# Normalised rows transposed by DMA on ScalarE's queue, and MLP pieces that run two behind the batch

## The chip, the cores and the metric

One core of a Trainium2 chip runs the kernel. The metric is the device time in microseconds of one execution, taken as the median of several runs; smaller is better.

## What is computed

Attention over 8 batches, 8 heads, 576 rows and 64 columns a head, with a causal mask and a bias from a running sum, and on its output a layer norm, a two-layer MLP with ReLU and a residual:

```python
scores = scale * q @ k.T
cum = cumsum(max(s, 0))
scores = where(causal, -1e9, scores + minimum(-(cum_i - cum_j), 0))
attn = softmax(scores)
x = concat_heads(attn @ v)                      # 8 x 576 x 512
xn = (x - mean(x)) / sqrt(var(x) + 1e-6) * g_ln
out = x + maximum(xn @ w_ch1, 0) @ w_ch2        # 512 -> 2048 -> 512
```

## The kernel before

**Slots.** The main loop runs over n = 0 to 63, one slot for each batch b = n // 8 and head h = n % 8. A slot computes the scores of its head (three PSUM banks `sa`, `sb`, `sc`, line 312, and for even h a small tile `sd`, line 347), takes their exponential on ScalarE into `er` (lines 323 and 358), masks on GpSimd (line 331), and then multiplies `er` of the head of two slots ago with V (`pv`, line 389, called by `pv_next`). The three score banks come from one PSUM pool of three buffers, so that the scores of a slot need the exponentials of the slot before to be done. VectorE divides by the row sums and writes the head's 64 columns into `xb` (512 rows of a batch) and `xm` (the last 64 rows, those of two batches in one 128-row tile).

**Normalisation.** When head 7 of a batch has gone through `pv`, which is in slot h=1 of the next batch, `ln_xn` (line 444) forms the normalised rows `xn` in bf16 for tiles t = 0 to 3 of 128 rows, and for odd batches for a fifth tile t = 4, the shared `xm`. The MLP needs them with the 512 columns on the partitions. `ln_tr` (line 478) does that: four TensorE transposes of 128x128 into a PSUM tile `trx` (line 484), and a copy by VectorE or ScalarE to `xT` or, for t = 4, `xTm` (lines 98 to 100). In slot h=2 of the next batch it handles tiles 0 and 1, in slot h=3 tiles 2, 3 and 4 (lines 822 to 827); for batch 7 it runs after the loop (line 842).

**MLP pieces.** `batch_units` puts 32 pieces of four matmuls of 512 columns each into a Python list `queue`: 16 of the first layer (`mlp1`, line 497; each ends in a ReLU to `hT` on ScalarE, or on VectorE for the first piece of a slot), then for each of four row tiles four quarters of the second layer (`mlp2`, line 515), of which the last ends in the residual sum `yo` on VectorE (line 524) and a DMA of 256 KB to the output on SyncE's queue (line 542). `run_units(n)` takes pieces from the list: in every slot one after the scores, one more after `sd`, and the rest after `pv`. The number per slot (line 809) is the length of the list over the slots to the next h=3, where the list is emptied (line 833) and the next batch's 32 pieces are put in. So the first layer takes slots h=4 to h=7, the second h=0 to h=3. A last chunk of 32 and some pieces handles the four `xm` tiles together.

**K and Q.** For batches 3 to 7, groups of four heads are loaded with SyncE's queue (`ld_rows`, line 164), cast on GpSimd (line 176) into 128-row tiles with the bias columns, and transposed into `kq` by five DMA transposes on SyncE's queue (`tr_rows`, line 186; the fifth has 64 rows). They are issued in slots h=4, 5 and 6 or h=0, 1 and 2 ahead of the group's first slot (h=0 or h=4). V is loaded on the same queue. The instructions of each engine and each issuing queue run in the order in which the program gives them; DMAs issued from SyncE and ScalarE rotate over eight completion semaphores, so each waits for the one issued eight before.

Of the kernel before, what the change touches and what calls it, by code (L numbers as in the profile page):

```python
# [15 lines left out]
P = 128  # L16
# [3 lines left out]
def kernel(  # L20
# [11 lines left out]
    nc = tc.nc  # L32
    B, H, S, D = q.shape
# [5 lines left out]
    NF = S // P  # L39
# [48 lines left out]
    xTm = const.tile([P, KD, 512], BF16, name="xTm")  # L88
# [7 lines left out]
    def copy_on(eng, out, in_):  # L96
        if eng == "act":
            nc.scalar.copy(out=out, in_=in_)  # L98
        elif eng == "dve":
            nc.vector.tensor_copy(out=out, in_=in_)  # L100
        else:
            nc.gpsimd.tensor_copy(out=out, in_=in_)  # L102
# [140 lines left out]
    def tr_pair(g):  # L243
        tr_kind("k", g)
        tr_kind("q", g)
# [29 lines left out]
    def qk_pair(g, k_engs, q_engs):  # L275
        tr_pair(g)
        evac_pair("k", g, k_engs)
        evac_pair("q", g, q_engs)
# [149 lines left out]
    xTs = {}  # L428
    xns = {}
# [48 lines left out]
    def ln_tr(b, t, eng="dve"):  # L478
        if (b, t) not in xns:
            return  # L480
        xn = xns.pop((b, t))
        tr = ps_t.tile([P, KD, P], BF16, name="trx", tag="tr")
        for kd in range(KD):
            nc.tensor.transpose(tr[:, kd, :], xn[:, kd * P : (kd + 1) * P], ident)  # L484
        if t < NF:
            dst = xTs[b][:, :, t * P : (t + 1) * P]
        else:
            dst = xTm[:, :, (b // 2) * P : (b // 2 + 1) * P]
        copy_on(eng, dst, tr)

    first_unit = [False]

    def mlp1(xT, fb):
# [60 lines left out]
    queue = []  # L554
    pend = []

    def run_units(n, dve_first=False):
        for i in range(n):
            if queue:
                first_unit[0] = dve_first and i == 0  # L560
                queue.pop(0)()
# [3 lines left out]
    def keep_warm(n):  # L565
        w = ps_t.tile([P, 512], F32, name="idle", tag="tr")
        for _ in range(n):
            nc.tensor.matmul(w, lhsT=zeros[:, 0:P], rhs=zeros, start=True, stop=True)
# [26 lines left out]
    for i in range(2):  # L595
# [5 lines left out]
        out=maskT,  # L601
        in_=maskT,
# [18 lines left out]
    for t in range(NT):  # L621
# [5 lines left out]
        out=c_in, in0=c_in, scalar1=0.0, scalar2=1.0 / scale, op0=ALU.max, op1=ALU.mult  # L627
    )
    nc.vector.tensor_tensor_scan(
        out=c_sc, data0=c_one, data1=c_in, initial=0.0, op0=ALU.mult, op1=ALU.add  # L630
# [44 lines left out]
    def pre(n):  # L675
        if n == 0:
            nc.vector.memset(mhalf, -0.5)
            ld_cast_pair(4)
        elif n == 1:
            ld_w1(1)  # L680
        elif n == 3:
            ld_cast_pair(5)
            for t in range(NT):
                ld_cast_v(1, t)
        elif n == 4:
            ld_w1(2)
            ld_w1(3)
        elif n == 7:
            ld_cast_pair(6)
            ld_w2(0)  # L690
            ld_cast_pair(7)
            ld_w2(1)
        elif n == 10:
            ld_w2(2)
            ld_w2(3)
        elif n == 12:
            nc.vector.memset(cT[:, :, 0, :, 0], -1.0)
            nc.vector.memset(cT[:, :, 1, :, 1:4], 1.0)
        elif n == 16:
            for r in rows:  # L700
                nc.gpsimd.memset(r[:, :, :, KA:P], 0.0)
        if n in PAIR_LOADS:
            ld_cast_pair(PAIR_LOADS[n])
        if n % 4 == 0 and 2 <= n // 4 + 1 < 2 * NPE:
            aug(n // 4 + 1, nc.sync)
        for gam in range(2 * NPE, NG):
            m = n - 4 * gam
            if m == -6:
                ld_rows(gam, 0), ld_rows(gam, 1)
            elif m == -5:  # L710
                cast_rows(gam, 0), cast_rows(gam, 1)
                ld_rows(gam, 2), ld_rows(gam, 3)
            elif m == -4:
                tr_rows(gam, 0), tr_rows(gam, 1)
                cast_rows(gam, 2), cast_rows(gam, 3)
                ld_rows(gam, 4)
            elif m == -3:
                tr_rows(gam, 2), tr_rows(gam, 3)
                cast_rows(gam, 4)
            elif m == -2:  # L720
                tr_rows(gam, 4)
        for nb in range(2, B):
            m = n - H * nb + (5 if nb == 2 else 7)
            if 0 <= m < NT:
                ld_v(nb, m)
            if 1 <= m <= NT:
                cast_v(nb, m - 1, "pool")

    def pv_next():
        pb, ph_ = pend.pop(0)  # L730
        pv(pb, ph_)
        if ph_ in (3, 5) or (ph_ == 7 and pb > 0):
            ln_stats(pb, ph_ // 2 - 1)
        elif pb == 0 and ph_ in (6, 7):
            ln_stats(0, ph_ - 4)
        if ph_ == 7:
            ln_open(pb)
            if pb == 0:
                ln_first()
                return  # L740
            for t in range({1: 3, B - 1: 1}.get(pb, NT)):
                ln_xn(pb, t)


    for n in range(BH):
        b, h = n // H, n % H
        pre(n)
        if n < 8:
            scores(b, h)
            if h in (1, 3, 5, 6):  # L750
                scores_d(b, h // 2)
            if h in (0, 2, 4):
                qk_pair(h // 2 + 1, ("dve", "dve"), ("act", "dve" if h < 4 else "act"))
            pend.append((b, h))
            if n == 7:
                pv_next()
                tr_pair(4)
                pv_next()
                evac_pair("k", 4, ("act", "act"))
                evac_pair("q", 4, ("act", "act"))  # L760
                trc = bias_tr()
                keep_warm(8)
                continue
            if n % 2 == 1 or n == 0:
                keep_warm(2)
            if n > 1:
                pv_next()
            if n == 6:
                pv_next()
            continue  # L770
        if n == 8:

            phs = [
                pool.tile([P, 512], F32, name="ph", tag=tag)
                for pool, tag in ((ps_m, "m"), (ps_m, "m"), (ps_s, "s"), (ps_s, "s"))
            ]

            def columns(t):
                cols = slice(t * P, (t + 1) * P)
                for fb, ph in enumerate(phs):  # L780
                    for kd in range(KD):
                        nc.tensor.matmul(  # L782
                            ph[:, cols],
                            lhsT=w1_bf[:, kd, fb * P : (fb + 1) * P],
                            rhs=xTs[0][:, kd, cols],
                            start=(kd == 0),
                            stop=(kd == KD - 1),
                        )

            for t in range(NF):  # L790
                ln_tr(0, t, "act" if t < 3 else "dve")
                if t > 0:
                    columns(t - 1)
            columns(NF - 1)
            for fb, ph in enumerate(phs):
                if fb % 2 == 0:
                    nc.scalar.activation(out=hT[:, fb, :], in_=ph, func=ACT.Relu)
                else:
                    nc.vector.tensor_scalar_max(out=hT[:, fb, :], in0=ph, scalar1=0.0)
            ln_first_rstd()  # L800
            queue += batch_units(0)[4:]
            scores(b, h)
            scores_d(b, h // 2)
            pend.append((b, h))
            run_units(1)
            continue

        end = next(m for m in (8 * i + 3 for i in range(2, B + 1)) if m >= n)
        nu = (2 if n < 16 else -(-len(queue) // (end - n + 1))) - 2
        if n in PAIRS:  # L810
            qk_pair(PAIRS[n], ("dve", "dve"), ("act", "act"))
        scores(b, h)
        run_units(1, True)
        if h % 2 == 0:
            scores_d(b, h // 2)
        run_units(1)
        if n > 9:
            pv_next()
        if n == 9:
            bias_rows(trc)  # L820
        pend.append((b, h))
        lt = {2: (0, 1), 3: (2, 3, 4)}.get(h, ()) if b > 1 else ()
        for t in lt:
            ln_tr(b - 1, t, "act" if b == 2 else "dve")
            if t != 1 and t != 4:
                run_units(1)
                nu -= 1
        if n == 2 * H + 2:
            for t in range(3, NT):
                ln_xn(1, t)  # L830
        run_units(nu)
        if b > 1 and h == 3:
            run_units(len(queue))
            queue += batch_units(b - 1)
    pv_next()
    run_units(3)
# [2 lines left out]
    for t in range(NT):  # L839
        ln_xn(B - 1, t + 1)  # L840
        run_units(1)
        ln_tr(B - 1, t, "act")
    run_units(len(queue))
    queue += batch_units(B - 1)
    queue += mixed_units()
# [30 lines left out]
```

## Time and profile before

| | |
|---|---|
| median of 5 runs | 368.45 us (368.0 to 368.88) |
| the profiled execution, its own time | 368.88 us |
| its span, first to last instruction | 367.2 us |
| granted TensorE clock | 1.00 |
| TensorE matmuls for the transposes of `xn` (line 484) | 144, on `trx` |
| copies out of `trx` | 23 on VectorE (415 ns), 13 on ScalarE (585 ns) |
| SyncE's DMA transposes into `kq` | 50, median issue 1.27 us |
| loop slots from n = 20 on, without a transpose of `xn` | 4.6 us each |

The profile is one execution as the hardware profiler recorded it. A row of the timeline gives start, duration, engine, source line, operation, output<-inputs, shape and count; brackets give the idle time of the engine before it and who ended it. PE is TensorE, PEld its weight loads, DVE VectorE, ACT ScalarE, POOL GpSimd, SP SyncE; a trailing q means the engine's queue that issues DMAs. Digits in the page's slices are the busy tenths of fortieths of the span. The landing of a DMA is read from the semaphore records of the trace: the last of its 16 increments.

### The profile page before, as it was taken

The numbers are of one execution on the slowest core, as the hardware profiler recorded it, in microseconds if no ns is written. First come the engines' busy times: TensorE is split into PE (matmuls) and PEld (weight loads), VectorE is DVE, ScalarE is ACT, GpSimd is POOL, SyncE is SP. The second block draws the span as 40 slices with busy tenths as digits, with TensorE's granted clock in tenths as the row PEclk, the third lists the DMA queues.
The fourth block names the chain that finished last, engine by engine and source line by source line (L and its number), as shares of the span: only waits on it lengthen the run. The fifth ranks groups of instructions, "written<-read, shape, count | busy, mean of one in ns | idle before, by whom it ended". The sixth has DMA issues, their size and how long they took to land.

```text
span 367.2 us, 8322 instructions
## 1 busy us (share of the span) xinstructions
PE 354.8 (97%) x3029; PEld 198.0 (54%) x3079; DVE 205.5 (56%) x539; ACT 194.2 (53%) x371; POOL 162.3 (44%) x441
## 2 busy tenths in 40 slices
PE   8898999999999999999999999999999999999995
PEld 3577565565555555555555555555555554444444
DVE  7597789795438453944385547743665483112211
ACT  5796988568743674357534753476337522501410
POOL 8864375748643746445744562555652101000000
PEclk9999999999999999999999999999999999999999
DMA  7999995579955989499969987798730011011013
GB/s 142 170 192 177 201 201 87 111 188 177 194 122 129 239 173 199 110 234 175 193 156 216 200 184 134 182 202 190 162 100 2 0 60 57 3 55 59 3 29 86
DMA packets 147981, 50.42 MB, mean 137 GB/s; under 512 B 134185, under 2 KB 143268, under 8 KB 147940
## 3 DMA queue, kind: packets, MB, share of 16 engines
q1 hardware_dynamic: 129364, 40.74, 51.2%
q0 software_dynamic: 18176, 8.62, 19.9%
q10 hardware_dynamic: 400, 0.52, 0.5%
q8 instruction: 24, 0.39, 0.4%
q14 instruction: 17, 0.14, 0.1%
HBM read 37.11 MB, written 9.44 MB: 127 GB/s over the span
## 4 chain that ended last, share of the span: by engine, by line
PE 84%; DVE 8%; ACT 3%; DMA 2%; issue 2%; ACTq 0%
PE ph L497 31%; PE py L515 30%; PE pot L389 7%; PE sc L312 4%; PE sa L312 3%; PE sb L312 3%; DVE xn L451 2%; PE trx L484 2%; DMA kq<-c 2%; DVE stats L423 1%; ACT er L323 1%; PE trqk L255 1%; ACT kq L98 1%; PE ph L782 1%; DVE xb L399 1%
## 5 line engine op out<-in xcount | busy, mean ns | idle before, releaser
L515 PE MATMUL py<-w_bf,hT 128*128 128x512 bf16 (+1 forms) x564 | 132.2, 373 | 1.6 <-DVE yo L524 0.4
L497 PE MATMUL ph<-xT,w_bf 128*128 128x512 bf16 x479 | 116.6, 379 | 1.1 <-DVE yo L524 0.2
L507 ACT ACTIVATE hT<-ph 128x512 bf16<-128x512 f32 x102 | 61.0, 598 | 62.8 <-PE ph L497 62.8
L515 PEld LDWEIGHTS <-hT 128*128 128x128 bf16 x592 | 53.5, 98 | 49.1 <-issue 0.9
L497 PEld LDWEIGHTS <-w_bf 128*128 128x128 bf16 x560 | 50.3, 97 | 51.7 <-issue 3.3
L323 ACT ACTIVATE er<-sa 128x512 bf16<-128x512 f32 x64 | 38.2, 597 | 70.4 <-PE sa L312 50.9
L331 POOL TENSOR_SCALAR_AFFINE_SELECT er<-er 128x128 bf16<-128x128 bf16 x216 | 59.4, 298 | 28.1 <-ACT er L323 28.0
L505 DVE TENSOR_SCALAR hT<-ph 128x512 bf16<-128x512 f32 x38 | 26.3, 692 | 54.6 <-PE ph L497 49.1
L176 POOL CAST rows<-rowtmp 128x512 bf16<-128x512 f32 (+1 forms) x50 | 30.5, 610 | 46.0 <-DMA rowtmp<-in_q_dram 42.8
L312 PEld LDWEIGHTS <-kq 68*128 68x128 bf16 x440 | 32.8, 97 | 26.6 <-DMA kq<-c 1.7
L389 PEld LDWEIGHTS <-er 128*128 128x128 bf16 x960 | 37.4, 98 | 14.2 <-issue 0.7
L389 PE MATMUL pot<-v_bf,er 128*128 128x65 bf16 x960 | 39.6, 193 | 0.3 <-PE sd L355 0.3
L323 ACT ACTIVATE er<-sc 128x512 bf16<-128x512 f32 x64 | 39.2, 613 | 0.0
L397 DVE RECIPROCAL rinv<-pot 128x5 f32<-128x5 f32 x64 | 12.3, 192 | 47.7 <-PE pot L389 47.4
L323 ACT ACTIVATE er<-sb 128x512 bf16<-128x512 f32 x64 | 38.4, 600 | 0.1
L524 DVE SCALAR_TENSOR_TENSOR yo<-py,rstd,xb 128x512 f32<-128x512 f32 x32 | 24.0, 748 | 25.5 <-PE py L515 18.6
L439 POOL TENSOR_TENSOR rstd<-rstd,mhalf 128x4 f32<-128x4 f32 (+1 forms) x8 | 8.8, 1097 | 44.7 <-DVE rstd L438 44.7
L399 DVE TENSOR_TENSOR xb<-pot,rinv 128x256 f32<-128x256 f32 x64 | 27.2, 425 | 2.2
L312 PE MATMUL sa<-kq 68*128 68x512 bf16 x64 | 24.4, 381 | 1.5 <-DMA kq<-c 1.2
L423 DVE BATCH_NORM_STATS2 stats<-xb 128x6 f32<-128x128 f32 (+2 forms) x100 | 25.3, 313 | 0.4
L312 PE MATMUL sc<-kq 68*128 68x256 bf16 (+1 forms) x208 | 25.2, 232 | 0.3
L102 POOL CAST v_bf<-vtmp 128x512 bf16<-128x512 f32 (+1 forms) x30 | 18.4, 614 | 14.5 <-DMA vtmp<-in_v_dram 13.2
(101 smaller groups left out, 331.4 us busy)
## 6 DMA issues: line engine op xcount, KB each, us to landing
out_dram<-yo SPq DMA_DIRECT2D x32, 256.0 KB
vtmp<-in_v_dram SPq DMA_DIRECT2D x24, 256.0 KB
rowtmp<-in_k_dram SPq DMA_DIRECT2D x40, 128.0 KB
rowtmp<-in_q_dram SPq DMA_DIRECT2D x40, 128.0 KB
w_bf<-in_moe_w_ch_dram POOLq DMA_DIRECT2D x8, 512.0 KB, 10.6
kp<-in_k_dram POOLq DMA_DIRECT2D x11, 144.0 KB, 6.1
qp<-in_q_dram POOLq DMA_DIRECT2D x11, 144.0 KB, 6.5
v_bf<-in_v_dram POOLq DMA_DIRECT2D x8, 128.0 KB, 8.5
```

Source lines behind the costliest of these rows:

```text
L176: nc.gpsimd.tensor_copy(out=r[0:pn, :, :, 0:D], in_=loaded.pop(("rows", gam, t))[0:pn])
L312: nc.tensor.matmul(a[:, c + a0 - q0 : c + a1 - q0], lhsT=k_cols(b, h, kb), rhs=cols, start=True, stop=not (pe_mask and diag),)
L323: nc.scalar.activation(out=e[:, o : o + 512], in_=a, func=ACT.Exp, scale=scale)
L331: nc.gpsimd.affine_select(out=e[:, o : o + P], in_=e[:, o : o + P], compare_op=ALU.is_ge, fill=0.0, base=0, pattern=[[1, P]], channel_mult ...
L389: nc.tensor.matmul(pot[:, t, :], lhsT=e[:, o : o + P], rhs=vv[:, kb, h, :], start=(kb == 0), stop=(kb == last),)
L399: nc.vector.tensor_tensor(out=xb[b][:, :, hs], in0=pot[:, 0:NF, 0:D], in1=rinv[:, 0:NF].unsqueeze(2).to_broadcast([P, NF, D]), op=ALU.mult,)
L423: nc.vector.bn_stats(out=st[b][:, t, part, :], in_=x[:, lo:hi])
L497: nc.tensor.matmul(ph, lhsT=w1_bf[:, kd, fb * P : (fb + 1) * P], rhs=xT[:, kd, :], start=(kd == 0), stop=(kd == KD - 1),)
L505: nc.vector.tensor_scalar_max(out=hT[:, fb, :], in0=ph, scalar1=0.0)
L507: nc.scalar.activation(out=hT[:, fb, :], in_=ph, func=ACT.Relu)
L515: nc.tensor.matmul(py[0], lhsT=hT[:, fb, t * P : (t + 1) * P], rhs=w2_bf[:, fb, c0:c1], start=(fb == 0), stop=(fb == FB - 1),)
L524: nc.vector.scalar_tensor_tensor(out=yo, in0=py[0], scalar=rs, in1=x[:, c0:c1], op0=ALU.mult, op1=ALU.add)
```

## The change

Tiles of batches 2 to 7 no longer go through TensorE: a new `ln_dma` takes an `xn` tile and issues one DMA transpose from ScalarE's queue, straight into `xT` or `xTm`. Batches 0 and 1 keep `ln_tr`. In the loop, tiles 0, 1 and 2 are issued at the end of slot h=2, tile 3 at the head of slot h=3 before its scores, tile 4 at the end of slot h=3; for batch 7, each tile is issued after the loop where its `ln_tr` was. In the built order of ScalarE's queue, tiles 0 to 3 stand together between the exponentials of h=2 and those of h=3, and tile 4 between those of h=3 and h=4. The pieces per slot are written out: four in each slot from n = 20, three in slots 23 and 27; the list is no longer emptied at h=3, so two second-layer pieces are left there and run first in slot h=4, and the first layer of the next chunk begins after that slot's `pv`.

```diff
+    def ln_dma(b, t):
+        if (b, t) not in xns:
+            return
+        if t < NF:
+            dst = xTs[b][:, :, t * P : (t + 1) * P]
+        else:
+            dst = xTm[:, :, (b // 2) * P : (b // 2 + 1) * P]
+        nc.scalar.dma_start_transpose(out=dst, in_=xns.pop((b, t)))
...
-        end = next(m for m in (8 * i + 3 for i in range(2, B + 1)) if m >= n)
-        nu = (2 if n < 16 else -(-len(queue) // (end - n + 1))) - 2
+        if n < 16:
+            nu = 2
+        elif n < 20:
+            nu = -(-len(queue) // (20 - n))
+        else:
+            nu = 3 if n in (23, 27) else 4
+        nu -= 2
+        if b > 2 and h == 3:
+            ln_dma(b - 1, 3)
...
-        lt = {2: (0, 1), 3: (2, 3, 4)}.get(h, ()) if b > 1 else ()
+        lt = {2: (0, 1), 3: (2, 3, 4)}.get(h, ()) if b == 2 else ()
         for t in lt:
-            ln_tr(b - 1, t, "act" if b == 2 else "dve")
+            ln_tr(b - 1, t, "act")
...
         run_units(nu)
+        if b > 2 and h == 2:
+            for t in range(3):
+                ln_dma(b - 1, t)
+        if b > 2 and h == 3:
+            ln_dma(b - 1, 4)
         if b > 1 and h == 3:
-            run_units(len(queue))
             queue += batch_units(b - 1)
...
         ln_xn(B - 1, t + 1)
         run_units(1)
-        ln_tr(B - 1, t, "act")
+        ln_dma(B - 1, t)
```

## The prediction

> **What bounds the kernel now.** I read the page's busy lines and slices first, then the chain of waits, TensorE's waits, the instruction groups by form, and last the timeline of one batch. The page:
>
> ```profile
> span 367.2 us, 8322 instructions
> PE 354.8 (97%) x3029; PEld 198.0 (54%) x3079; DVE 205.5 (56%) x539; ACT 194.2 (53%) x371; POOL 162.3 (44%) x441
> PE   8898999999999999999999999999999999999995
> ACT  5796988568743674357534753476337522501410
> DMA  7999995579955989499969987798730011011013
> ...
> PE 84%; DVE 8%; ACT 3%; DMA 2%; issue 2%; ACTq 0%
> ```
>
> TensorE is full in every slice from the sixth on, and no other engine is. TensorE's waits (who, for whom, us, times, longest) come to under 6 us in the whole span, mostly in the start:
>
> ```profile
> PE sa L312 <- DMA kq<-c: 1.2, 1, 1.2
> PE sd L347 <- ACT kq L98: 0.6, 2, 0.4
> PE trx L484 <- DVE xn L451: 0.5, 2, 0.3
> PE py L515 <- DVE yo L524: 0.4, 2, 0.2
> ```
>
> So a TensorE instruction taken out of the loop or the tail is time gained, unless what replaces it makes TensorE wait. The work in question, by form (count | busy us, mean ns | idle before), and SyncE's existing transposes (min/median/max ns):
>
> ```profile
> L484 PE MATMUL trx<-ident,xn 128*128 128x128 bf16 x144 | 13.8, 219 | 0.6 <-DVE xn L451 0.5
> L100 DVE COPY xT<-trx 128x512 bf16<-128x512 bf16 x21 | 8.1, 417 | 2.0 <-PE trx L484 1.6
> L98 ACT COPY xT<-trx 128x512 bf16<-128x512 bf16 x11 | 6.4, 585 | 14.3 <-PE trx L484 14.2
> ...
> L186 SPq DMA_TRANSPOSE kq<-rows x50: 1218/1274/2228, 83.0 to 267.5; - x50
> ```
>
> 219 ns is a pipelined duration; the rate is what counts. The timeline of batch 5 (slot h=2 starts at 186.28, h=3 at 191.36):
>
> ```profile
> 186.28 0.38 PE L312 MATMUL sa<-kq 68*128 68x512 bf16 x1
> ...
> 188.20 0.27 ACT L358 ACTIVATE er<-sd 64x128 bf16<-64x128 f32 x1
> ...
> 191.36 0.38 PE L312 MATMUL sa<-kq 68*128 68x512 bf16 x1
> ...
> 191.62 1.22 SPq L186 DMA_TRANSPOSE kq<-rows  x1
> ...
> 191.84 0.60 ACT L323 ACTIVATE er<-sa 128x512 bf16<-128x512 f32 x1 [3.36 <-PE sb L312]
> ...
> 194.21 0.39 PE L484 MATMUL trx<-ident,xn 128*128 128x128 bf16 x4
> ...
> 194.43 1.03 PE L515 MATMUL py<-w_bf,hT 128*128 128x512 bf16 x4
> ```
>
> Four transposes of one tile cost 194.43 - 194.21 = 0.22 us of TensorE. The slots agree: 4.63 us for even h and 4.58 for odd without such tiles, but h=2 takes 5.08 with two tiles (+0.45), h=3 5.02 with two (+0.44) and 5.62 with three (+1.04, of which 0.67 is the tiles and 0.37 is waiting, for DVE's yo among it). The bracket in ACT's row at 191.84 says that ACT had been idle 3.4 us: in h=2 and h=3 it has little but its exponentials.
>
> **What the Trainium skill says.** Page "DMA: Bandwidth & Descriptors", section "DMA Transpose (X-bar)", on two transposing streams in flight: transposes issued from SP and from ACT must not overlap; the later stream's first must wait for the earlier one's full completion. In the changed program's order ACT's first transpose of each batch does wait for SP's last kq transposes, and SP's next one for ACT's last. Only SP transposes in the kernel before, so its trace doesn't show the price. Same page, "Issuing engines are not separate DMA queues": all queues share the 16 DMA engines, so ACT's queue adds load and no bandwidth. The trace agrees in that transfers land later when the engines are full: SP's kq transposes land 2.7 to 5.7 us after issue.
>
> **The change part by part.**
>
> TensorE, removed: 4+5+4+5+4 tiles of batches 2 to 6 and 5 of batch 7, 27 tiles, 108 transposes: 27 x 0.223 = 6.0 us, all on the bound engine. With them go waits: 0.37 us in each of the two three-tile slots of that length (h=3 of batches 4 and 6) and 0.07 in the tail. Together 0.8; I count half, since yo still queues behind DVE's normalisation: 0.4.
>
> DVE, removed: 22 evacuations x 0.415 = 9.1 us, from the slots where it also normalises. ACT, removed: 5 x 0.585 in the tail. Neither bounds; they count only through the half of the waits above.
>
> ACT, added: 27 transpose issues, each of 4 column blocks of 128. SP's issue of 8 blocks takes 1.27 us, with 64 rows as with 128, so blocks set it; its plainest copy (out) takes 0.33 us. If the issue is all blocks, 0.63; if 0.33 is fixed, 0.33 + 4 x 0.117 = 0.80; if the count of blocks doesn't matter, 1.27. I take 0.75, ends 0.63 and 1.27. A value below nothing is excluded, since it is new work on this queue. What matters is the in-order queue: behind the four transposes stand the exponentials of slot h=3, and for these TensorE waits, since scores of h=4 reuse their three PSUM banks. In batch 5, counted from h=2's start T2 = 186.28: ACT ends h=2's exponentials at T2+2.2, xn of tiles 0 to 3 ends at +1.3, +2.3, +3.2, +4.1. ACT's first issue waits for SP's transpose of the group's last 64 rows. Before, that one was issued only at T2+5.3, because SP stood behind an output write that waited for yo. In the new order the output write ahead of it is one whose yo is made before the normalisation, since the MLP runs half a slot later; then SP's own work sets it: two transposes from T2-2.8 to T2-0.1, one v load and one write, then issue at about T2+1.1, landing 2.7 us later, T2+3.8. Then 0.3 for the several waits and 4 x 0.75: ACT is free at T2+7.1. Exponentials of h=3 would start at T3+0.48 = T2+5.1 in a slot of 4.6, so they lag 2.0 us. The third one ends at T3+2.05 today and its bank is wanted at T3+5.0: 2.95 us of slack. Cost nothing, by 0.95 us. If that cover is gone, each us beyond it costs a us a batch, five times. The fifth tile (odd batches) goes out behind h=3's exponentials with 0.75 and delays h=4's by no more than what ACT's idle 3 us absorb.
>
> Landing of xT: the fourth tile is issued by T2+7.1, lands 3 to 5 us later, at the latest T2+12.1. First use is the first MLP-1 piece, now after two pieces and the PV of h=4: T2+9.2+3.2 = T2+12.4. Just hidden at the long end; at 3 us by 2 us. In the tail: xn of tile 3 ends at 301.8 before, issue and landing give 305.5; 15 pieces of 0.86 us from the last PV at 294.3 last until 307.3. Hidden.
>
> SP: nothing is added, but its next rows and transposes wait for ACT's landings (to T2+10). Before, SP's first kq transpose of the next group went at T2+17.3 in batch 4 (163.6 against 147.96) through the yo block, and the group's last landed 1.0 us ahead of its use. SP loses the block of up to 5.7 us and gains a wait that is shorter: nothing, most likely some slack. POOL: same instructions.
>
> DMA engines: 27 x 128 KB in 256-byte packets, 512 each, 13,824. The 129,364 packets of SP's queue took 51.2% of 367.2 us on 16 engines, 23 ns each, so an estimated 20 us of all 16: mean share from 72% to some 78%. Loads have slack in slots, so I count nothing; it lengthens landings.
>
> Pacing: every slot from 20 on still runs four pieces of 0.86 us (three in 23 and 27, which leaves two behind), 32 a batch, so TensorE's sum is the same. ReLU pieces move half a slot away from the transposes: the cover for ACT's issue.
>
> Sum, against the profiled execution: 368.88 (span 367.2 and 1.7 around it) - 6.0 - 0.4 = 362.5. The median of the runs, 368.45, is 0.43 below it: 362.1.
>
> **The rivals.** (1) Partly eaten: the issue costs about 1.0 us, or SP's last transpose lands 1 us later than worked out; ACT is free at T2+8.1, lag 3.0, and every fuller batch oversteps: 0.5 to 0.8 us in each of five, 3 us back: about 365. For it: an SP issue took up to 2.2 us when the DMA engines were full. Against: that was for twice the blocks.
>
> (2) No change: issue at SP's full 1.27 us. ACT is free at T2+9.2, lag 4.1, overstepped by 1.15 in five batches = 5.8 us: 367.9, no change by the bound below; 0.1 us more a batch and it is 368.4.
>
> (3) Slower: ACT's queue blocks behind SP's landing. Its place is the first transpose of each batch; if SP's last kq transpose lands 5.0 instead of 2.7 us after issue (the longest of the 128-row ones is 5.7), because the DMA engines now carry more, and issues cost 1.0, ACT is free at T2+10.4, lag 5.3, and TensorE stalls for a bank by 5.3 - 2.95 = 2.35, 11.8 us in five batches: 362.1 + 11.8 = 373.9. (xT, landing later too, is wanted later by the same stall.) It decides from a delay of 2.25 us beyond my T2+7.1 on: then 1.3 us x 5 pays back the 6.4. For it: both queues are in order and wait for each other. Against: the 64-row transposes, which are the ones waited for, landed within 2.7 to 3.0 us in all ten groups.
>
> **How the numbers follow.** Forecast 0.62 at 362.1 (own range 361.2 to 364); rival 1 0.14; rival 2 0.06; rival 3 0.18. Faster by over 0.2%, about what this measurement can tell from no change: 0.62 + 0.14 = 0.76; within it 0.06; slower 0.18. The range goes from 361.0 (all waits gone, 0.4 better, and some more) to 370.5, which takes in rivals 1 and 2 and the near part of 3; some 0.15 is left above and 0.04 below.
>
> **What would show it.** Right: 36 instead of 144 transposes on TensorE, slots h=2 and h=3 of batches 3 to 7 at 4.6 us; ACT's transposes near 0.75 us each, its exponentials of h=3 late by some 2 us and TensorE's waits still under 1 us per batch; SP's last small transpose issued before ACT needs it. Wrong: TensorE waits at scores of h=4 for ACT, or at MLP-1 pieces for a DMA into xT, or at the next group's scores for kq; issues of 1.2 us or more on ACT; a tail that waits for batch 7's landing.

## The result: the gain on TensorE came, and was given back with more

| | before | after |
|---|---|---|
| median | 368.28 us (46 runs, 367.57 to 370.3) | 370.58 us (26 runs, 367.20 to 374.04) |
| after / before, 95% interval | | 1.0051 [1.0037, 1.0065] |
| the profiled execution, its own time | 368.88 | 372.53 |
| its span | 367.2 | 370.8 |

So 2.3 us slower where 6.4 us faster was forecast, at the upper end of the range, 370.5. The ratios here and below compare fast runs alone: five of the 26 runs after, 373.0 to 374.0 us, count as slow, and by the ratio the kernel is 1.9 us slower. The kernel after also spreads more, 6.8 us against 2.7. The profiled executions differ by 3.65 us, more than the medians; the sums below are made against them.

The page of the kernel after, busy lines and slices:

```profile
span 370.8 us, 8187 instructions
PE 352.5 (95%) x2924; PEld 192.8 (52%) x2971; DVE 196.4 (53%) x517; ACT 191.3 (52%) x366; POOL 161.6 (44%) x441
PE   8898999999999999989997999999989999999995
PEclk9999999999999999999999999999989999999999
DMA  8999994679999999999899899999730033001003
```

The slices that had stood at 9 without a break from the sixth to the last but one now have three holes: an 8 in the 18th (158 to 167 us), a 7 in the 22nd (195 to 204) and an 8 in the 30th (269 to 278). Those are the slots h=3 and h=4 of batches 4, 5 and 7. TensorE's waits (who, for whom, us, times, longest) name two that weren't there:

```profile
PE sa L312 <- ACT er L323: 3.9, 3, 2.4
PE ph L507 <- DMA xT<-xn: 2.4, 2, 1.6
```

Both are on the list of signs under which the forecast is wrong: scores of h=4 that wait for ScalarE's exponentials, and first-layer pieces that wait for a transposed tile. (Line 507 is `mlp1`, 497 in the kernel before; the change shifts what follows it by ten lines and more.) What is behind the first stands in the answer for line 499, the new DMA transposes on ScalarE's queue (count, then min/median/max ns of one issue):

```profile
L499 ACTq DMA_TRANSPOSE xT<-xn x24: 1204/1234/1408, 111.2 to 304.9; - x24
L499 ACTq DMA_TRANSPOSE xTm<-xn x3: 1231/1237/1267, 155.3 to 306.3; - x3
```

An issue of four column blocks takes 1.23 us, as long as SyncE's of eight.

**Where the time went, batch by batch.** Most slots are as forecast: 4.63 and 4.58 us, h=2 and h=3 with the rest. I measured each slot from its first score to the next slot's and took the excess over that. T2 is again the start of slot h=2, and the batch is that of the slot; the tiles belong to the batch before it.

| batch | ScalarE issues tiles 0 to 3 | exponentials of h=3 start | tile 3 lands | excess, us | what TensorE waited for |
|---|---|---|---|---|---|
| 3 | T2+2.1 to 7.5 | T2+7.6 | T2+12.4 | 1.28 | the tile, at the first piece of `mlp1` |
| 4 | T2+3.0 to 8.6 | T2+8.7 | T2+14.5 | 2.44 | the tile |
| 5 | T2+5.8 to 11.1 | T2+11.2 | T2+13.7 | 3.12 | score bank, so ScalarE |
| 6 | T2+2.1 to 7.4 | T2+7.5 | T2+11.5 | 0.18 | next to nothing |
| 7 | T2+4.6 to 9.9 | T2+10.0 | T2+11.0 | 1.89 + 1.69 | score bank; 1.69 is put down to a halved clock, below |

Together 10.6 us. With 6.0 us of transposes and 0.8 us of waits gone, 367.2 - 6.8 + 10.6 = 371.0, against a span of 370.8.

Batch 5 in the timeline (start, us, engine, line, operation; brackets: idle before, releaser; T2 = 185.65, h=3 starts at 190.28, h=4 at 197.45):

```profile
186.66 2.74 SPq L186 DMA_TRANSPOSE kq<-rows  x1
190.28 0.38 PE L312 MATMUL sa<-kq 68*128 68x512 bf16 x1
191.41 5.29 ACTq L499 DMA_TRANSPOSE xT<-xn  x4
196.81 0.60 ACT L323 ACTIVATE er<-sa 128x512 bf16<-128x512 f32 x1 [8.96 <-POOL v_bf L102]
197.45 0.38 PE L312 MATMUL sa<-kq 68*128 68x512 bf16 x1 [2.43 <-ACT er L323]
```

Read it from the top. SyncE's last `kq` transpose of the group needs 2.74 us to issue (min 1.2) and lands at T2+5.6. Only then does ScalarE issue its four, 5.29 us without a break: in every batch of the trace its first transpose starts only after SyncE's last one has landed, here by 0.2 us. ScalarE has done nothing else for 8.96 us, yet the exponentials of h=3, whose scores have lain ready since about 191, start at 196.81: 6.05 us later than the T2+5.1 of an undisturbed slot. The forecast's rule for what that costs was lag less 2.95 us of bank slack: 3.10, and the slots of this batch are 3.12 us too long. In batch 7 it gives 4.84 - 2.95 = 1.89, and 1.89 is left of the 3.58 measured there when the clock's 1.69 is taken off.

Batch 4 is the other kind; its lag of 3.6 us would cost 0.6, but the tile lands later still, and TensorE waits for it:

```profile
160.93 1.89 PE L507 MATMUL ph<-xT,w_bf 128*128 128x512 bf16 x8 [1.63 <-DMA xT<-xn]
```

And in batch 7, behind a gap of 1.23 us on TensorE at 273.23, the clock halved. Three stretches of that time (busy time per engine with counts, then granted clock, DMA share, GB/s):

```profile
273.50:275.30 1.80, 1.52 (x12) 0.82 (x12) 0.00 (x0) 1.80 (x5) 1.22 (x6) 1.00 0.00 0
275.35:278.76 3.41, 3.41 (x25) 1.75 (x24) 1.36 (x3) 0.55 (x2) 0.95 (x4) 0.50 0.01 2
278.80:280.50 1.70, 1.70 (x12) 0.81 (x11) 0.28 (x1) 0.85 (x2) 0.00 (x0) 1.00 0.41 154
```

TensorE is fully busy for 3.41 us and gets through half the work: an estimated 1.7 us lost. It is the 8 in the PEclk slices.

### The profile page after: what moved, and what is told of

The parts are those of the page before. It is cut to its first block, busy times and chain, and to the rows that moved or that the text cites. A ratio compares the mean times of both kernels' runs of the same rounds, so it can differ in the third digit from the quotient of the medians.

```text
span 370.8 us, 8187 instructions
## 1 busy us (share of the span) xinstructions
PE 352.5 (95%) x2924; PEld 192.8 (52%) x2971; DVE 196.4 (53%) x517; ACT 191.3 (52%) x366; POOL 161.6 (44%) x441
## 3 DMA queue, kind: packets, MB, share of 16 engines
q0 software_dynamic: 18176, 8.62, 20.5%
## 4 chain that ended last, share of the span: by engine, by line
PE 79%; DVE 6%; DMA 6%; ACT 3%; POOL 2%; issue 2%; ACTq 1%; POOLq 0%
PE ph L507 30%; PE py L525 30%; PE pot L389 6%; DMA xT<-xn 4%; PE sc L312 3%; PE sb L312 3%; PE sa L312 3%; DMA v_bf<-in_v_dram 2%; ACT er L323 2%; DVE stats L423 1%; POOL v_bf L147 1%; DVE xb L399 1%; DVE kq L100 1%; ACT kq L98 1%; ACTq L499 1%
## 5 line engine op out<-in xcount | busy, mean ns | idle before, releaser
L312 PE MATMUL sb<-kq 68*128 68x64 bf16 (+1 forms) x168 | 24.4, 246 | 0.6 <-ACT hT L807 0.2
```

Of the source, the lines that this page charges most:

```text
L312: nc.tensor.matmul(a[:, c + a0 - q0 : c + a1 - q0], lhsT=k_cols(b, h, kb), rhs=cols, start=True, stop=not (pe_mask and diag),)
```

## Experiments

The theories, as the expectations name them. **A**: each DMA transpose holds ScalarE's in-order queue for about 1.23 us whatever its size, so four in a row push the exponentials and the landing of `xT` too late. **B**: the queues wait for each other; SyncE's landing, late under full DMA engines, starts ScalarE late. **C**: the new order of the MLP pieces costs the time. **D**: SyncE's own queue falls behind. All ratios are against runs of the kernel before on the same chip (368.13 to 368.62 us).

| kernel | us (range) | ratio, 95% |
|---|---|---|
| before + new pacing only | 367.45 (366.86 to 369.76) | 0.9972 [0.9959, 0.9986] |
| DMA transposes only | 389.45 (387.4 to 391.15) | 1.0566 [1.0535, 1.0597] |
| four tiles a transpose, ScalarE | 366.37 (362.23 to 369.84) | 0.9924 [0.9904, 0.9944] |
| two tiles a transpose, ScalarE | 363.37 (363.05 to 363.65) | 0.9861 [0.9838, 0.9884] |
| four tiles a transpose, SyncE | 375.42 (374.79 to 376.99) | 1.0179 [1.0148, 1.0211] |
| one tile a transpose, SyncE | 388.43 (386.71 to 392.24) | 1.0536 [1.0493, 1.058] |
| transposes split over h=2 and h=3, pieces four behind | 387.45 (386.25 to 389.99) | 1.0508 [1.0473, 1.0544] |
| two tiles a transpose, pieces four behind | 381.25 (378.94 to 384.62) | 1.0333 [1.0282, 1.0385] |
| one tile a transpose, `kq` rows a slot earlier | 366.19 (363.78 to 367.34) | 0.994 [0.9919, 0.9961] |
| two tiles a transpose, `kq` rows a slot earlier | 362.23 (361.54 to 363.1) | 0.984 [0.9814, 0.9865] |

### The two halves of the change, each alone

Pacing alone: the kernel before, all transposes on TensorE, with the change's lines for `nu` in place of the old two, and without the emptying of the list at h=3.

> The pieces two behind, the transposes left on TensorE. Theory A (each DMA transpose holds ScalarE's in-order queue for 1.23 us whatever its size, so four in a row push the exponentials and the landing of xT late) and theory B (the waits between the two transposing queues and the full DMA engines make xT late, the issue time doesn't matter) both expect no change: 367.9 to 368.8 us, TensorE's slots from n = 24 on at 4.6 us plus 0.22 a tile. Theory C (the order of the pieces costs) expects 370 us or more.

Measured: 367.45 us, faster by 0.3%, a little below the no change that A and B expected. The three-tile slots h=3 of batches 4 and 6 shrink from 5.62 to 5.25 us, 0.74 us together, which is the waiting in them that the forecast saw there. C falls: the order of pieces costs nothing and brings a little, 0.7 us.

DMA alone: the kernel after, with the old `nu` and the list emptied at h=3 again.

> The DMA transposes with the old pacing: the list is emptied at h=3 and the first layer begins with the first piece of h=4, some 2.5 us earlier than in the changed kernel. A and B expect that TensorE waits for xT in all five batches, 2 to 3 us more each: 378 to 385 us. C expects that it is no slower than the changed kernel: 370 us or less.

Measured: 389.45 us, slower than either theory said, and for another reason than both had. TensorE's longest wait isn't for `xT`:

```profile
PE sb L312 <- DMA kq<-rows: 14.6, 5, 4.1
```

Batch 5 in its timeline (h=4's first score at 202.38) shows how:

```profile
196.41 5.22 ACTq L499 DMA_TRANSPOSE xT<-xn  x4
...
197.58 0.36 SPq L552 DMA_DIRECT2D out_dram<-yo  x1
...
202.82 1.20 SPq L186 DMA_TRANSPOSE kq<-rows  x1
...
205.62 0.61 PE L312 MATMUL sb<-kq 68*128 68x64 bf16 x3 [2.87 <-DMA kq<-rows]
```

Without the half slot, the output write ahead of SyncE's last `kq` transpose waits for a `yo` that comes too late, and in the built order this transpose stands behind ScalarE's four: in batch 5 the last of them lands at 202.75, and SyncE, idle since 197.94, issues at 202.82. It issues at T2+8.6 to T2+12.9 and lands 2.1 to 4.4 us after the group's first use in all five batches. The gaps are followed by halved clock for 20.5 us in all, up to 10 us lost. So the two halves belong together: the half slot puts SyncE's last transpose ahead of ScalarE's, as the forecast had it, and without it the DMA half costs 21 us instead of 2.

### Fewer issues on ScalarE's queue

If A holds, what counts is how many transposes are issued, not how large they are. Two kernels put several tiles into one transpose; `xn` tiles lie side by side, and `xT` is laid out tile by tile. Otherwise they are the kernel after.

```diff
-        xTs[b] = xtp.tile([P, KD, 512], BF16, name="xT", tag="xT")
+        xTs[b] = xtp.tile([P, NF, KD, P], BF16, name="xT", tag="xT")
...
-        nc.scalar.dma_start_transpose(out=dst, in_=xns.pop((b, t)))
+        if t == NF:
+            nc.scalar.dma_start_transpose(out=xTm[:, b // 2], in_=xns.pop((b, t)))
+        elif t % 2 == 2 - 1:
+            nc.scalar.dma_start_transpose(
+                out=xTs[b][:, t + 1 - 2 : t + 1].rearrange("p t k s -> p (t k) s"),
+                in_=xg.pop((b, t // 2)).rearrange("p t c -> p (t c)"),
+            )
...
-                rhs=xT[:, kd, :],
+                rhs=xT[:, :, kd, :],
```

With 4 for 2 throughout (the `xn` tiles are then allocated by four) it is one transpose of 16 blocks a batch:

> The changed kernel with tiles 0 to 3 of a batch in one DMA transpose of 16 column blocks (xT laid out by tile), issued where tile 3 was: one issue in place of four, the same bytes, the same waits between the queues. A expects an issue near 1.3 to 2.5 us, ScalarE's exponentials of h=3 late by 1 to 2 us, no wait of TensorE for them, and 362 to 364 us. B expects the stalls to remain: 368 to 371 us.

Two tiles, eight blocks:

> The same with two tiles in one DMA transpose of 8 blocks: two issues a batch. A expects about half way, 364 to 367 us, issue again near 1.24 us as SP's of 8 blocks. B expects 368 to 371 us.

Measured: 366.37 and 363.37 us. The first lies between what A and B expected, the second 0.6 us below A's range. The same bytes, moved by the same queue in the same slots, cost 7.2 us less in two pieces than in four. The new layout isn't what brings it: undisturbed slots still take 4.63 and 4.58 us. The issues of the pair and of the four:

```profile
L507 ACTq DMA_TRANSPOSE xT<-xn x12: 1247/1272/1937, 110.6 to 294.9; - x12
```

```profile
L507 ACTq DMA_TRANSPOSE xT<-xn x6: 1334/1614/3658, 112.7 to 297.5; - x6
```

Eight blocks take 1.27 us, 0.04 more than four. With two issues instead of four the exponentials of h=3 start at T2+5.2 to T2+6.4, and at T2+8.2 in batch 5; TensorE's only stall of note in these batches is 1.3 us in batch 5, for `xT` (landed at T2+13.7), where SyncE's last `kq` transpose had landed at T2+4.8. One issue of 16 blocks is better than four, but no better than two: it must wait for all four tiles, takes 1.3 to 3.7 us, and all of `xT` lands at T2+8.8 to T2+14.9. That is A with a limit: up to eight blocks the issue has one price, and at 16 a longer issue and a late landing take its place.

### The transposes on SyncE's queue

If ScalarE's queue is the trouble, SyncE's is the rival place: ScalarE is left alone, and no two queues have to wait for each other. The transposes move from one queue to the other in the kernels with four tiles (two calls, one for tile 4) and with one tile a transpose (one call):

```diff
-            nc.scalar.dma_start_transpose(
+            nc.sync.dma_start_transpose(
```

> Tiles 0 to 3 in one DMA transpose, and tile 4, issued from SyncE's queue in place of ScalarE's, so that all transposes stand in one queue: no wait of ScalarE for a landing, no issue on ScalarE. Theory A (what hurts is the time that ScalarE's in-order queue stands, by issues and waits) expects no bank stall, and 362 to 364 us unless xT, issued behind SyncE's own loads, lands after its use. A rival D (SyncE's queue, issuing 80% of the time already, falls behind, and kq or xT is late) expects 366 us or more, with waits of TensorE for a DMA into xT or kq.

> The changed kernel with its 27 transposes tile by tile on SyncE's queue: 4 to 5 issues of 1.24 us a batch more there. A expects 362 to 366 us. D expects clearly more than the version with one transpose a batch on SyncE: 368 us or more.

Measured: 375.42 and 388.43 us. In both, the exponentials of h=3 start at T2+5.1 in every batch, as if undisturbed, and no score of these batches waits for ScalarE, so the stalls at the scores are indeed ScalarE's transposes. But now `xT` comes too late. TensorE's waits with four tiles and with one:

```profile
PE ph L518 <- DMA xT<-xn: 10.5, 4, 4.6
```

```profile
PE ph L507 <- DMA xT<-xn: 17.6, 4, 6.0
```

Four waits, in batches 3 to 6; batch 7, when SyncE has no more loads to issue, has none. D is right of SyncE, though its queue isn't simply full: in batch 4 with four tiles the last `xn` is done at T2+4.5, but SyncE issues nothing from T2+3.4 to T2+6.4, waiting with an output write, then that write and five loads, and the transpose only at T2+9.5. The half of the change that went to ScalarE's queue was the better half of a choice between two busy queues.

### Later pieces, for more time to land

Two pieces more are left behind at h=3 (slots 21 and 22 also take three), to give the tiles 1.7 us more; the first kernel also spreads the issues:

```diff
-            nu = 3 if n in (23, 27) else 4
+            nu = 3 if n in (21, 22, 23, 27) else 4
...
-        if b > 2 and h == 3:
-            ln_dma(b - 1, 3)
...
         if b > 2 and h == 2:
-            for t in range(3):
+            for t in range(2):
                 ln_dma(b - 1, t)
         if b > 2 and h == 3:
-            ln_dma(b - 1, 4)
+            for t in range(2, NT):
+                ln_dma(b - 1, t)
```

> The changed kernel with the same 27 issues on ScalarE, but tiles 0 and 1 between the exponentials of h=2 and h=3 and tiles 2 to 4 between those of h=3 and h=4, with the pieces four behind, so that xT may land later. A (five us of issues in one place exceed the slack of 2.95 us; the sum over the batch would fit) expects no bank stall in most batches and 362 to 365 us. B (waits between the queues and landings) expects no gain: 368 us or more.

The second is the kernel with two tiles a transpose, with the line of `nu` alone:

> Two tiles in one transpose on ScalarE as before, but the pieces four behind, so that the first layer begins with h=5. If only xT's landing were left to gain, 361.5 to 363 us, without a wait for xT. If the half slot also matters because the output write ahead of SyncE's last kq transpose then waits for a yo that is made behind the normalisation, more than with two behind: 365 us or more, with SyncE's last transpose of a group 3 to 5 us later and ScalarE waiting for it.

Measured: 387.45 and 381.25 us. Both fell into the trap of the DMA half alone. TensorE's waits in the second:

```profile
PE sb L312 <- DMA kq<-rows: 7.3, 8, 1.5
```

The later pieces move `yo` and with it SyncE's write, and the last `kq` rows land 0.6 to 1.9 us after the first scores of slot h=4, in all five batches; in the first kernel it is 6.2 us of the same wait, in six places. These waits are some 8 of the 18 us that the second kernel lost; the rest is in smaller waits that I didn't take apart. In the first kernel the exponentials of h=3 do start at T2+5.1 to T2+7.0, inside the slack, but those of h=4 start 2 to 6 us into their slot. It therefore doesn't tell whether spreading the issues helps; that stays open. The second kernel says that two pieces behind is not a loose number: two more cost 18 us.

### SyncE's landing out of the way

B's term by itself: the last 64 `kq` rows are loaded and cast one slot earlier, and transposed right behind tiles 2 and 3, so that SyncE is done before ScalarE wants to begin. Once on the kernel after, once on the one with two tiles a transpose:

```diff
                 ld_rows(gam, 2), ld_rows(gam, 3)
+                ld_rows(gam, 4)
             elif m == -4:
...
                 cast_rows(gam, 2), cast_rows(gam, 3)
-                ld_rows(gam, 4)
             elif m == -3:
-                tr_rows(gam, 2), tr_rows(gam, 3)
                 cast_rows(gam, 4)
-            elif m == -2:
+                tr_rows(gam, 2), tr_rows(gam, 3)
                 tr_rows(gam, 4)
```

> The changed kernel, tile by tile, with the same earlier kq transposes: the wait between the queues is taken away, the issues stay. Theory A alone (issues: 4 x 1.23 us) expects ScalarE free at T2+7.5 in every batch, a lag of 2.4 us, inside the banks' slack of 2.95, but xT's last tile landing at or after its use at T2+12.1: 365 to 369 us. Theory B alone (the wait for SyncE's landing) expects that all is gained: 362 to 363 us. Both together: the bank stalls of batches 5 and 7 (5 us) go and some wait for xT stays, 364 to 366 us.

> Two tiles in one transpose on ScalarE, two behind, and the last 64 rows of each kq group loaded one slot earlier and transposed right behind tiles 2 and 3, ahead of the v load and the output write. What is left against the floor in the pair version is batch 5's wait of ScalarE for that landing (to T2+4.8) and xT behind it, 1.6 us. Expected: ScalarE's first issue at T2+2.2 in all batches, no TensorE wait over 0.5 us after n = 24, 361.5 to 362.5 us. If the landing is late for another reason (full DMA engines), no gain: 363 to 364 us.

Measured: 366.19 us tile by tile, 4.4 less than after with the issues unchanged, so B's term is real; B alone (362 to 363 us) falls. The time lies in A's range and 0.2 us above that of both together, and the wait is not wholly gone: ScalarE's first issue stands at T2+2.1 to 2.2 in three batches, but at 4.3 in batch 5, behind SyncE's landing at 4.0, and at 3.5 in batch 7, so that the score bank still stalls in both (1.6 and 0.8 us by the slots; the rule gives 1.5 and 0.8).

With both terms treated it is 362.23 us, faster than the kernels before and after. There ScalarE's first issue came at the expected T2+2.2 in batch 3 alone, and at 2.7 to 4.0 in the others. The page of this last kernel:

```profile
span 360.5 us, 8177 instructions
...
PE 350.5 (97%) x2943; PEld 191.8 (53%) x2971; DVE 196.1 (54%) x517; ACT 191.1 (53%) x366; POOL 160.0 (44%) x441
PE   8998999999999999999999999999999999999995
PEclk9999999999999999999999999999999999999999
```

and its batch 5 (T2 = 181.66, h=3 at 186.30, h=4 at 190.88):

```profile
185.33 2.90 ACTq L507 DMA_TRANSPOSE xT<-xn  x2
186.30 0.38 PE L312 MATMUL sa<-kq 68*128 68x512 bf16 x1
188.33 0.60 ACT L323 ACTIVATE er<-sa 128x512 bf16<-128x512 f32 x1 [4.47 <-POOL er L331]
190.88 0.38 PE L312 MATMUL sa<-kq 68*128 68x512 bf16 x1
...
194.13 1.90 PE L518 MATMUL ph<-xT,w_bf 128*128 128x512 bf16 x8 [0.18 <-DMA xT<-xn]
```

ScalarE issues from T2+3.7 to T2+6.6; the exponentials lag 1.6 us, inside the bank slack; h=4's scores wait for nothing, and the first `mlp1` piece waits 0.18 us. The span is 6.7 us below that of the kernel before, but 0.7 of that lies ahead of slot n = 20, where nothing was changed (the 1.2 us wait for `kq<-c` on the prediction's list isn't in this trace). From n = 20 on it is 6.0 us, in round numbers 6.0 of the transposes and 0.8 of waits, less 0.7 given back in slots that run 0.2 to 0.4 us over in batches 4, 5 and 6.

## Why the prediction was wrong

**The step that failed is the issue on ScalarE's queue**: "I take 0.75, ends 0.63 and 1.27". It was formed by scaling SyncE's 1.27 us for eight blocks to four, because 64 rows took as long as 128; but every transpose of the kernel before has eight blocks, so its profile says nothing of the blocks. Measured is 1.23 us, the upper end, the one with the words "if the count of blocks doesn't matter". The 0.48 us missing four times make 1.9 us a batch between the first issue and the exponentials. An estimate from the batch table: with issues of 0.75 us from the measured starts, and the same 0.35 us between them, ScalarE would have been free by T2+5.4 to T2+9.1, and only batch 5 would overstep its slack, by some 1.1 us where 3.1 and 1.9 were measured in two. That the number of issues carries the result is shown by the pair: two instead of four, with the same bytes in the same place, 370.58 to 363.37 us. SyncE's landing is the second term, 4.4 us by itself; both together bring 8.4, less than their sum, since either one shortens the same stalls.

The rest, point by point:

- *TensorE, 6.0 us removed*: right. 36 matmuls on `trx` are left of 144, and the kernel with hardly a stall is 6.0 us shorter from n = 20 on. The waits gone with them are 0.7 us in the run with the pacing alone, not the 0.4 counted.
- *Each us of lag beyond 2.95 costs a us*: right, to 0.02 us in the two batches where a bank was the wait (in one after the clock's 1.69 us, an estimate, is taken off). *Five times*: wrong; it was two batches, 5.0 us together.
- *SyncE's last transpose lands at T2+3.8*: near the average, but not right batch by batch: the landings stand at T2+1.4 to T2+5.6. ScalarE's first issue stood at T2+2.1 in two batches, 3.0, 4.6 and 5.8 in the others. The landing 2.7 us after issue, taken from ten groups before, became 4.6 in batch 5, with an issue of 2.7 in it. This is the mechanism of the rival "ScalarE's queue blocks behind SyncE's landing", and with SyncE's rows a slot earlier 4.4 us come back. The rival was right on the mechanism, at 0.18, and priced it too evenly: 2.35 us in five batches where 3.1 and 1.9 came in two.
- *The half slot puts SyncE's last transpose ahead*: right, and more needed than the prediction says. Without it the change costs 21 us.
- *xT lands 3 to 5 us after its issue, by T2+12.1, first used at T2+12.4, "just hidden"*: wrong at both ends. Tiles 2 and 3 of batches 3 and 4 took 5.9 to 7.3 us from the start of their issue, and tile 3 landed at T2+12.4 and T2+14.5. And the first use is at T2+12.3 only from batch 4 on; slot 27 has three pieces, so batch 3 wants its tiles at T2+11.25. The two differences, 1.2 and 2.2, are the excess of these batches (1.28 and 2.44) within 0.3. A cover called "just hidden" by 0.3 us at its long end should have entered the sum with a price.
- *No change at 1.27 us a tile*: the rival that had the right issue time gave 367.9 to 368.4. It counted the banks alone (5.8 us, measured 5.0) and left the landing of `xT` (3.7 in batches 3 and 4) and the clock (1.7) out.
- *DMA load*: right. ScalarE's queue carries 14,688 packets more (13,824 worked out) and its share rises from 0.5% to 6.1% of the engines' span (some 5.4 worked out). "I count nothing" for what it does to landings was the slip, as above. That the load alone lengthened them is not shown, since no run took it away by itself.
- *SyncE nothing or slack*: right. The last `kq` landing before use grew from 1.0 to 2.4 us before to 2.3 to 7.5, but for one group with 0.01 (and the first, which had 5.9 and has 4.8). The 163.6 us of the working is T2+15.7 in batch 4, not T2+17.3; nothing rests on it. *The tail hidden*: right.
- The halved clock was in nobody's list.

## What to carry to other kernels

On an engine that also computes, the DMA transpose was priced here by the issue, and up to eight column blocks issues counted, not bytes: put as much into one as its landing allows, and look what stands behind it in that engine's queue. Where two queues took turns, the second inherited every delay of the first, so first clear the turn (an earlier load) and then add the work. And a cover that is "just enough" by the median row became a cost in the batches where an issue or a landing came late.

## What the runs showed of the hardware

- **The issue of a DMA transpose hardly depends on its size**, up to eight column blocks of 128: medians 1.23 us for four and 1.27 for eight on ScalarE's queue, 1.26 for four and 1.26 to 1.29 for eight on SyncE's. For 16 it was 1.61 (ScalarE) and 2.6 us (SyncE, up to 4.1). Single issues were longer at any size, up to 2.2 us for four blocks and 2.8 for eight; what lengthened them no run isolates. The Trainium skill, page "DMA: Bandwidth & Descriptors", section "Issuing engines are not separate DMA queues", calls the time on the sequencer "usually small relative to the DMA itself"; in the kernel after 1.2 us stand against 2.3 to 7.3 us from the start of the issue to the landing, and the issue is what other work waits behind. The measurement decides.
- **Halved clock after short gaps.** The granted clock was 0.5 for 3.41 or 6.83 us, beginning in a gap of TensorE or up to 2.1 us after it: once in the kernel after (gap 1.23), four times with the DMA half alone (2.8 to 4.1), three times with one tile a transpose on SyncE (2.9 to 6.0). Not after every gap: 2.43 us at 197.45 in the kernel after was followed by none, nor was 3.53 us at 123.5 in the last of these kernels. The page "TensorE: Matmul & The Clock Gate", section "What's actually happening", has the half clock after at least one idle window of about 3.4 us; the length of the window agrees, but 1.23 us of gap were enough here once, and 3.53 were not. What decides between the gaps no run isolates. Such a window of 3.41 us, busy throughout, costs an estimated 1.7 us on top of the gap.
